# A quarter of w_in loaded earlier and scaled one gate sooner, and two idle matmuls taken out

## The chip, the cores and the metric

The kernel runs on one core of one Trainium2 chip. The metric is the time of one execution on the device in microseconds (us). Six runs of the kernel before gave a median of 107.75 us (107.39 to 110.95; without the highest, 107.39 to 107.86).

## The reference

Two layers follow each other. The first is an attention without softmax: q and k (4 batches, 4 heads, 1088 rows, 32 values) are each projected twice to 8 values, and the outer product of the two projections gives 64 features. The second is a layer with a Swish activation whose slope `beta` differs by hidden unit.

```python
def phi(x):
    a = einsum('rd,bhsd->bhsr', S1, x)
    b = einsum('rd,bhsd->bhsr', S2, x)
    return einsum('bhsi,bhsj->bhsij', a, b).reshape(..., 64)
kv  = einsum('bhsf,bhsd->bhfd', phi(k), v)
z   = sum(phi(k), axis=2)
num = einsum('bhsf,bhfd->bhsd', phi(q), kv)
den = einsum('bhsf,bhf->bhs', phi(q), z)[..., None] + 1e-6
x   = (num / den)            # heads joined: 4352 tokens x 128
h   = x @ w_in               # 128 x 2048
out = (h * (1 / (1 + exp(-beta * h)))) @ w_out   # 2048 x 128
```

The kernel uses that h * sigmoid(beta*h) is silu(beta*h) / beta: it multiplies the columns of w_in by beta and the rows of w_out by 1/beta, and then only needs a plain silu.

## The kernel before

The attention is worked batch by batch. k and q are loaded in rows and transposed in 32x32 blocks on VectorE (`turn_k`, line 378, and `turn_q`, line 384), projected on TensorE, multiplied out to features on VectorE or GpSimd (`outer`, line 441), and summed against v on TensorE (`kv`, line 536). The results for the tokens go as fp16 into `xT`. The second layer then takes tokens in chunks: the first two are of 256 tokens, the others of 512. A "wave" (`w1`, line 332) multiplies one chunk by some columns of the scaled w_in (`winp`), and ScalarE turns the result into `g` with silu; `w2` (line 308) multiplies `g` by the scaled w_out (`woutp`) into `moeout`. With 256 tokens a wave takes 512 columns of winp, that is two slices of 256.

The order on every engine is the order in which the code stands: nothing is reordered by a scheduler. Batch 0 goes first, in code written out by hand (lines 675 to 736), and its q in two parts: "chunk A" is the first 16 of 34 groups of rows, `QA0`, and "chunk B" the other 18. From line 828 a string `SEQ` lists the rest step by step. It begins with `W aB c1 V c0 w4 bB W`: a wave, the spread of chunk B by S1 (`a_B`, line 739), the copy of half of it by ScalarE (`c1`), four matmuls of `w2` (`V`), the other copy, two scalings of w_out, and the spread by S2 (`b_B`).

All large loads are issued by SP's queue in the order of lines 164 to 177. w_in and w_out are loaded in halves. `load_rows(q, ..., ((QA0, T),))` is the second part of q in batch 0, which `turn_q(0, QA0, T)` at line 720 transposes. VectorE has it in its queue ahead of `invert`, which gives the reciprocal `rc` of the denominators of chunk A.

w_in is scaled by GpSimd in slices of 256 columns (`prep_win`, line 257), w_out by ScalarE or GpSimd. GpSimd is held back by "gates" (`gate`, line 671): a copy of one column that waits for a tile of VectorE's. The first gate waits for the last k features of batch 0 (`KP`); one slice follows. The second waits for `rc`; the other seven slices follow.

`keep_warm(n, t)` (line 180) issues n matmuls of 512 columns on a constant tile, whose result nobody reads. In `a_B` two of them write the second of the two PSUM tiles of the spread that comes after. The tiles of tag "wave" turn over two buffers; `nps`, the numerators of chunk A, has the buffer that the first tile of `a_B` takes next.

Of the kernel before, what the change touches and what calls it, by code (L numbers as in the profile page):

```python
# [18 lines left out]
def kernel(  # L19
# [18 lines left out]
    DFF = moe_w_in.shape[1]  # L38
# [3 lines left out]
    T = S // 32  # L42
# [44 lines left out]
    def cut(t, ap, extra=0):  # L87
        return bass.AP(tensor=t.tensor, offset=t.offset + extra, ap=[list(t.ap[0])] + ap)
# [25 lines left out]
    k_t, q_t, v_t = {}, {}, {}  # L114

    def load_rows(src, dst, b, tag, parts=((0, T),)):
        if b not in dst:
            dst[b] = ld.tile([P, T, D], F32, tag=tag, name=tag)
        for t0, t1 in parts:
            nc.sync.dma_start(  # L120
                out=dst[b][:, t0:t1, :],
                in_=bass.AP(
                    tensor=src.tensor,
                    offset=src[b, 0].offset + t0 * D,
                    ap=[[T * D, P], [1, (t1 - t0) * D]],
                ),
            )


    def load_v(b):  # L130
        t = v_t[b] = ld.tile([P, H, NJK, D], F32, tag="v", name="v")
        if b < B - 1:
            for h in range(H):
                nc.sync.dma_start(
                    out=t[:, h],
                    in_=bass.AP(
                        tensor=v.tensor, offset=v[b, h].offset, ap=[[T * D, 32], [NJK * D, 4], [1, NJK * D]]
                    ),
                )
            return  # L140
        nc.gpsimd.memset(t[:, :, NJK - 2 :, :], 0.0)
        for g in range(4):
            nj = min(NJK, T - NJK * g)
            nc.sync.dma_start(
                out=t[g : P : 4, :, :nj],
                in_=bass.AP(
                    tensor=v.tensor,
                    offset=v[b, 0].offset + NJK * g * D,
                    ap=[[T * D, 32], [S * D, H], [1, nj * D]],
                ),  # L150
            )

    def load_win(c0, c1):
        nc.sync.dma_start(out=w_in_sb[:, c0:c1], in_=moe_w_in[:, c0:c1])

    def load_wout(j0, j1):
        nc.sync.dma_start(
            out=w_out_sb[:, j0:j1, :],
            in_=moe_w_out[j0 * P : j1 * P, :].rearrange("(j p) m -> p j m", p=P),
        )  # L160

    K_PARTS = ((0, 18), (18, T))
    QA0 = 2 * q_chk[0][1]
    load_rows(k, k_t, 0, "k", K_PARTS)
    load_rows(q, q_t, 0, "q", ((0, QA0),))
    load_v(0)
    load_wout(0, NJ // 2)
    load_win(0, DFF // 2)
    load_rows(q, q_t, 0, "q", ((QA0, T),))
    load_rows(k, k_t, 1, "k")  # L170
    load_win(DFF // 2, DFF)
    load_wout(NJ // 2, NJ)
# [7 lines left out]
    def keep_warm(n, t=None):  # L180
        if t is None:
            t = pso.tile([P, TCH], F32, tag="moeout", name="warm")
        for _ in range(n):
            nc.tensor.matmul(out=t, lhsT=idle, rhs=cut(idle, [[0, 4], [1, P]]), start=True, stop=True)  # L184
# [72 lines left out]
    def prep_win(c0, c1, eng=None):  # L257
        (eng or nc.gpsimd).tensor_tensor(  # L258
            out=winp[:, c0:c1], in0=w_in_sb[:, c0:c1], in1=beta_bc[:, c0:c1], op=MUL
        )  # L260
# [129 lines left out]
    PS, KP, QO, QT, QP, ND, KAB, QAB, ASB, KVZ, KVD, RB, WZ = ({} for _ in range(13))  # L390

    def wave2(name):
        return psm.tile([P, 2, 512], F32, tag="wave", name=name)

    def two(name):
        return ps2.tile([P, 2, 512], F32, tag="two", name=name)

    def one(name):
        return ps1.tile([P, 512], F32, tag="one", name=name)
# [62 lines left out]
    def spread(which, n, dsts):  # L462
        t0, tn = q_chk[n]
        for c in range(2):
            for m in range(2):
                for pr, dst in enumerate(dsts):
                    h = 2 * pr + m
                    rows = slice(32 * h, 32 * h + 32)
                    nc.tensor.matmul(  # L469
                        out=dst[64 * c : 64 * c + 64, m, : 32 * tn],  # L470
                        lhsT=(sa if which == "a" else sb_)[rows, :],
                        rhs=qT2[0][rows, t0 + c * tn : t0 + c * tn + tn, :],
                        start=True,
                        stop=True,
                    )
# [195 lines left out]
    def gate(t):  # L671
        g = sbA.tile([P, 1], F32, tag="gate", name="gate")
        nc.gpsimd.tensor_copy(out=g, in_=t[:, :1])
# [40 lines left out]
    kvd0 = sb([P, 2, F], F32, "kvd0")  # L714
    nc.scalar.copy(out=kvd0, in_=cut(KVZ[0], [[0, 2], [1, F]]))
    gate(KP[0][:, NJK - 1, H - 1])
    prep_win(0, 256)
    dps = one("dps")
    den0(0, dps)
    turn_q(0, QA0, T)  # L720
# [7 lines left out]
    keep_warm(1, nps[:, 0])  # L728
    num0(0, nps)
    keep_warm(2)  # L730
    for c in range(256, DFF, 256):
        prep_win(c, c + 256)
    for j in range(NJ // 2):
        prep_wout_act(j)
# [3 lines left out]

    def a_B():
        PS["a"] = [wave2("aps"), two("aps")]  # L740
        keep_warm(2, PS["a"][1][:, 0])
        spread("a", 1, PS["a"])

    def b_B():
# [46 lines left out]
    for nm, fn in (("aB", a_B), ("bB", b_B), ("dB", d_B), ("iB", i_B), ("nB", n_B)):  # L791
        DO[nm] = fn
# [76 lines left out]
```

## Time and profile before

| | |
|---|---|
| profiled execution, time | 107.39 us |
| its span, first to last instruction | 105.2 us |
| median of six runs | 107.75 us |
| TensorE busy | 95.9 us (91%) |
| ScalarE busy | 78.0 us (74%) |
| VectorE busy | 66.4 us (63%) |
| GpSimd busy | 26.2 us (25%) |
| mean granted TensorE clock | 0.989 |
| DMA engines busy | nearly full from 4 to 24 us |

Busy time is an average over stages with different limits. The chain of work that ended last follows the program back from its last instruction, at each step to what released it; what stands on it sets the end. The timeline lists the instructions in order of time, and the idle time in front of each, with what ended it. In all views PE is TensorE, PEld its loading of weights, DVE VectorE, ACT ScalarE, POOL GpSimd and SP the queue that issues the loads; `L258` is line 258 of the kernel.

### The profile page before, as it was taken

Reading aid. Unit: us, or ns where it says so; the run is one execution under the profiler, and the core shown is the slowest. Engines: PE = TensorE matmul, PEld = TensorE weight load, DVE = VectorE, ACT = ScalarE, POOL = GpSimd, SP = SyncE. Lnnn points to the kernel's source line nnn. Section 1 sums busy time; section 2 is a strip of 40 time slices with the busy share of each in tenths; the row PEclk is TensorE's granted clock in tenths of the full one; section 3 lists DMA queues with packets and bytes.
Section 4 is the critical chain, followed back from the end, with each engine's and each line's share of the span. In section 5 each row is a group of like instructions: output and inputs, shape, how many; then the busy total and the mean of one; then the engine's idle time right before and its main releaser. Section 6 shows DMA issues by size and latency. Waiting matters only on the chain.

```text
span 105.2 us, 2880 instructions
## 1 busy us (share of the span) xinstructions
PE 95.9 (91%) x1175; PEld 46.0 (44%) x1175; DVE 66.4 (63%) x131; ACT 78.0 (74%) x102; POOL 26.2 (25%) x37
## 2 busy tenths in 40 slices
PE   5778999898979999999999999999899999999930
PEld 2224724355556543534445353346353444445720
DVE  5568998599899935997999564789935200200210
ACT  0648069939897966779977299899892999999920
POOL 5320149640089300400760063008300000000000
PEclk9999999999999999999999999999999999999995
DMA  2999999980002300037800462410014041023043
GB/s 60 310 252 310 363 373 376 418 292 21 6 12 38 55 5 0 6 58 136 329 6 9 81 143 85 82 18 6 0 25 75 0 76 30 0 41 62 15 85 50
DMA packets 24580, 11.33 MB, mean 108 GB/s; under 512 B 18900, under 2 KB 23028, under 8 KB 24568
## 3 DMA queue, kind: packets, MB, share of 16 engines
q1 hardware_dynamic: 23808, 11.05, 37.6%
q8 instruction: 9, 0.15, 0.6%
q10 hardware_dynamic: 696, 0.09, 0.6%
q0 software_dynamic: 64, 0.02, 0.1%
q14 instruction: 3, 0.02, 0.1%
HBM read 8.93 MB, written 2.23 MB: 106 GB/s over the span
## 4 chain that ended last, share of the span: by engine, by line
PE 62%; ACT 17%; DVE 11%; DMA 4%; issue 2%; DVEq 0%; ACTq 0%
PE wave L341 19%; PE moeout L316 19%; ACT g L350 17%; PE kvz L539 5%; PE nps L655 4%; DMA beta<-in_moe_beta_dram 4%; PE kps L406 3%; PE bps L469 2%; PE yps L510 2%; PE aps L469 2%; PE qps L406 1%; DVE rb L614 1%; DVE qT L385 1%; PE betaps L247 1%; DVE xT L634 1%
## 5 line engine op out<-in xcount | busy, mean ns | idle before, releaser
L350 ACT ACTIVATE g<-wave 128x1024 f16<-128x1024 f32 x68 | 65.1, 1037 | 12.0 <-PE wave L341 11.7
L341 PE MATMUL wave<-xT,winp 128*128 128x512 f16 (+1 forms) x160 | 39.7, 347 | 1.3 <-DVE xT L634 0.8
L316 PE MATMUL moeout<-g,woutp 128*128 128x512 f16 (+1 forms) x160 | 38.6, 347 | 0.3 <-ACT g L350 0.3
L341 PEld LDWEIGHTS <-winp 128*128 128x128 f16 x160 | 14.5, 98 | 17.6 <-issue 7.3
L316 PEld LDWEIGHTS <-woutp 128*128 128x128 f16 x160 | 15.0, 97 | 16.1 <-issue 3.5
L326 DVE STREAM_TRANSPOSE o_sb<-moeout 128x512 f32<-128x512 f32 (+1 forms) x10 | 6.2, 620 | 19.6 <-PE moeout L316 19.6
L445 POOL TENSOR_TENSOR qo<-qab 128x512 f32<-128x512 f32 (+1 forms) x7 | 11.0, 1590 | 20.4 <-DVE qab L534 20.4
L445 POOL TENSOR_TENSOR kp<-kab 128x512 f32<-128x512 f32 (+1 forms) x5 | 6.2, 1248 | 16.8 <-DVE kab L428 9.5
L445 DVE TENSOR_TENSOR kp<-kab 128x512 f32<-128x512 f32 (+2 forms) x11 | 8.9, 821 | 0.0
L456 DVE STREAM_TRANSPOSE qt<-qo 128x512 f32<-128x512 f32 (+1 forms) x12 | 8.6, 743 | 0.0
L666 DVE CAST xT<-nps 128x576 f16<-128x576 f32 x5 | 3.8, 758 | 5.6 <-PE nps L655 2.8
L379 DVE STREAM_TRANSPOSE kT<-k 128x1088 f32<-128x1088 f32 (+2 forms) x5 | 5.3, 1067 | 1.1 <-DMA k<-in_k_dram 1.1
L184 PE MATMUL warm<-idle 128*128 128x512 f16 x13 | 4.9, 514 | 1.1 <-DVE idle L96 1.1
L445 DVE TENSOR_TENSOR qo<-qab 128x512 f32<-128x512 f32 (+1 forms) x5 | 5.8, 1192 | 0.1
L258 POOL TENSOR_TENSOR winp<-w_in_sb,beta_bc 128x256 f16<-128x256 f32 x8 | 5.6, 730 | 0.0
L385 DVE STREAM_TRANSPOSE qT<-q 128x1088 f32<-128x1088 f32 (+2 forms) x5 | 5.3, 1065 | 0.4 <-DMA q<-in_q_dram 0.4
L539 PE MATMUL kvz<-kp,v 128*32 128x64 f32 x288 | 5.5, 221 | 0.0
L539 PEld LDWEIGHTS kvz<-kp,v 128*32 128x32 f32 x288 | 4.3, 110 | 2.5 <-issue 1.5
L273 ACT ACTIVATE woutp<-w_out_sb,rbeta 128x128 f16<-128x128 f32 x16 | 5.1, 396 | 0.0
L655 PE MATMUL nps<-qt,nd 32*32 32x288 f32 x192 | 4.8, 412 | 0.0
L428 DVE STREAM_TRANSPOSE kab<-kps 128x288 f32<-128x288 f32 x8 | 3.4, 461 | 1.7 <-PE kps L406 1.7
L486 DVE TENSOR_TENSOR qp<-bps,asb 128x512 f32<-128x512 f32 (+1 forms) x4 | 2.8, 720 | 1.6 <-PE bps L469 1.6
(84 smaller groups left out, 66.9 us busy)
## 6 DMA issues: line engine op xcount, KB each, us to landing
v<-in_v_dram SPq DMA_DIRECT2D x15, 144.0 KB, 4.5
k<-in_k_dram SPq DMA_DIRECT2D x3, 544.0 KB, 7.0
q<-in_q_dram SPq DMA_DIRECT2D x3, 544.0 KB, 7.2
w_out_sb<-in_moe_w_out_dram SPq DMA_DIRECT2D x2, 512.0 KB, 7.7
w_in_sb<-in_moe_w_in_dram SPq DMA_DIRECT2D x2, 512.0 KB, 7.8
out_dram<-o_sb SPq DMA_DIRECT2D x16, 64.0 KB, 1.9
out_dram<-o_sb SPq DMA_DIRECT2D x10, 32.0 KB, 1.6
k<-in_k_dram SPq DMA_DIRECT2D x1, 288.0 KB, 3.2
```

The source lines that it names most:

```text
L258: (eng or nc.gpsimd).tensor_tensor(out=winp[:, c0:c1], in0=w_in_sb[:, c0:c1], in1=beta_bc[:, c0:c1], op=MUL)
L273: nc.scalar.activation(out=woutp[:, j, :], in_=w_out_sb[:, j, :], func=ACTF.Copy, scale=rbeta[:, j : j + 1])
L316: nc.tensor.matmul(out=moe["acc"][:, :tw], lhsT=woutp[:, j, :], rhs=g[jj], start=(j == 0), stop=(j == NJ - 1),)
L326: nc.vector.transpose(out=o_sb[:, :nt, :].rearrange("p t d -> p (t d)"), in_=moe["acc"][:, :tw])
L341: nc.tensor.matmul(out=wv[:, jj // per, o : o + tw], lhsT=winp[:, (j0 + jj) * P : (j0 + jj + 1) * P], rhs=xT[:, t0 : t0 + tw], start=True, ...
L350: nc.scalar.activation(out=g[:, :, :gw], in_=wv[:, :, :gw], func=ACTF.Silu)
L379: nc.vector.transpose(out=kT2[b % 2][:, t0:t1].rearrange("p t s -> p (t s)"), in_=k_t[b][:, t0:t1].rearrange("p t d -> p (t d)"),)
L385: nc.vector.transpose(out=qT2[b % 2][:, t0:t1].rearrange("p t s -> p (t s)"), in_=q_t[b][:, t0:t1].rearrange("p t d -> p (t d)"),)
L445: (eng or nc.vector).tensor_tensor(out=cut(dst[b][:, j0:j1], [[F, n], [R, R], [1, R]]), in0=cut(src[b][:, 0, j0:j1], [[R, n], [1, R], [0, ...
L456: nc.vector.transpose(out=QT[b][:, j0:j1].rearrange("p j h c s -> p (j h c s)"), in_=QO[b][:, j0:j1].rearrange("p j h f -> p (j h f)"),)
L539: nc.tensor.matmul(out=KVZ[b][32 * h : 32 * h + 32, :F], lhsT=v_t[b][:, h, j, :], rhs=KP[b][:, j, h, :], start=(j == 0), stop=(j == NJK - ...
L655: nc.tensor.matmul(out=tiles[g // 2][32 * h : 32 * h + 32, g % 2, :JW], lhsT=ND[b][rows, fc, 32 * h : 32 * h + 32], rhs=QT[b][rows, :, h, ...
```

## The change

There are three edits. In the list of loads, the first half of w_in is cut in two quarters. The first quarter is issued right after v of batch 0, then the second part of q, then the first half of w_out, then the second quarter of w_in. The loads behind these keep their order, and SP issues one load more. At the first gate, GpSimd scales two slices instead of one, and the loop behind the second gate begins one slice later. In `a_B` the two idle matmuls are taken out.

```diff
@@ the loads
     load_v(0)
+    load_win(0, DFF // 4)
+    load_rows(q, q_t, 0, "q", ((QA0, T),))
     load_wout(0, NJ // 2)
-    load_win(0, DFF // 2)
-    load_rows(q, q_t, 0, "q", ((QA0, T),))
+    load_win(DFF // 4, DFF // 2)
     load_rows(k, k_t, 1, "k")
@@ the gate on the k features
     gate(KP[0][:, NJK - 1, H - 1])
-    prep_win(0, 256)
+    for c in (0, 256):
+        prep_win(c, c + 256)
     dps = one("dps")
@@ behind the gate on rc
-    for c in range(256, DFF, 256):
+    for c in range(512, DFF, 256):
         prep_win(c, c + 256)
@@ a_B
         PS["a"] = [wave2("aps"), two("aps")]
-        keep_warm(2, PS["a"][1][:, 0])
         spread("a", 1, PS["a"])
```

## The prediction

> **What bounds the kernel now.** I read the chain of work that ended last first, because it says which stage a saving would have to reach the end from.
>
> ```profile
> PE 62%; ACT 17%; DVE 11%; DMA 4%; issue 2%; DVEq 0%; ACTq 0%
> ```
>
> TensorE carries most of it; ScalarE's 17% is the tail (from 83.16 to 100.69 the chain is one activation after another), and VectorE's 11% lies before 30 us. Both edits lie before 20 us, so next comes the same chain in order of time, there:
>
> ```profile
> 15.58 0.44 DVE xT L634
> 16.02 0.04 issue
> 16.06 0.60 PE wave L341 x4
> 16.66 0.43 PE aps L184 x2
> 17.09 0.90 PE aps L469 x14
> 17.99 0.54 PE moeout L316 x4
> 18.53 1.00 PE bps L469 x12
> ...
> 19.62 0.77 DVE qp L486
> ```
>
> The two idle matmuls that the change removes (`aps L184 x2`) stand on the chain with 0.43 us. That is what they occupy, not yet what they cost. Third, the timeline of that stretch (start, duration, instruction, and in brackets the idle time before it and what ended it):
>
> ```profile
> 12.92 0.73 POOL L258 TENSOR_TENSOR winp<-w_in_sb,beta_bc 128x256 f16<-128x256 f32 x1
> 13.23 0.77 DVE L385 STREAM_TRANSPOSE qT<-q 128x576 f32<-128x576 f32 x1
> 14.05 0.45 DVE L604 STREAM_TRANSPOSE dT<-dps 128x256 f32<-128x256 f32 x1
> 14.53 0.18 DVE L607 TENSOR_SCALAR rc<-dT 128x16 f32<-128x16 f32 x1
> 15.06 0.18 POOL L673 COPY gate<-rc 128x1 f32<-128x1 f32 x1 [1.41 <-DVE rc L608]
> 15.20 4.84 POOL L258 TENSOR_TENSOR winp<-w_in_sb,beta_bc 128x256 f16<-128x256 f32 x7
> 16.39 0.42 DVE L634 TENSOR_TENSOR xT<-nps,rb 128x256 f16<-128x256 f32 x1
> 17.02 0.97 PE L469 MATMUL aps<-qT,s 32*64 32x288 f32 x16
> 18.03 1.18 ACT L480 COPY asb<-aps 128x576 f32<-128x576 f32 x2 [0.22 <-PE aps L469]
> ```
>
> GpSimd stands idle for 1.41 us ahead of the gate on rc. The transpose of q's second part starts with no idle time before it, and the first wave on the chain is released by xT, not by a scaled slice. Last, the windows, for the clock:
>
> ```profile
> 7.90:11.50 3.60, 3.25 (x92) 2.04 (x91) 3.23 (x7) 2.14 (x5) 0.00 (x0) 1.00 0.99 304
> 16.06:19.62 3.56, 3.56 (x44) 1.83 (x44) 1.94 (x3) 3.34 (x8) 3.56 (x6) 1.00 1.06 392
> ```
>
> The seventh figure is the granted clock: 1.00 in both, and the DMA engines beside it are full.
>
> [...] the 128x576 transpose took 772 ns with a GpSimd slice over its first half and 778 ns at 3.95 us with GpSimd idle. On tensor_scalar the trace shows nothing, since none meets a slice. [...] The window 7.90 to 11.50, without one idle matmul, kept 1.00[...].
>
> **The change part by part.** Sums are made against the profiled execution (107.39 us, span 105.2, so 2.19 outside it); it is the lowest of the six, 0.36 under the median of 107.75.
>
> *The idle matmuls.* They go (0.43 us, 16.66 to 17.09). What is late next is a buffer. The first matmul of a_B's spread writes the "wave" buffer that nps held, and nps is read until the second divide ends, 16.39 + 0.42 = 16.81. From the first divide to its wave took 15.58 + 0.42 = 16.00 to 16.06, so 0.06; the spread can then start at 16.87 instead of 17.02. That gives 0.15 of the 0.43; the rest becomes a wait. Behind the spread: the copy c1 on ScalarE (18.03, 0.02 after the spread) comes 0.15 earlier, at 17.88, ScalarE being free at 17.81. The four moeout matmuls need g, which ends at 17.81, so with the same 0.05 or so they move from 17.92 to 17.87, only 0.05. The bps spread follows them. Its second matmul waited for c1 in this execution; in the timeline the sixteen took 1.00 us against 0.97 for the same sixteen of aps, so the wait cost 0.03. The bps spread thus ends 0.05 + 0.03 = 0.08 to 0.09 us earlier and qp on VectorE starts at about 19.53 instead of 19.62. Bounds: 0 (all given back in waits) and 0.15 (the copy alone decides); I take 0.09. From 19.62 to 30 us the chain runs through VectorE and TensorE without a DMA, then TensorE is full, so 0.09 reaches the end.
>
> *The second slice at the kp gate.* No work is added: one 0.73 us slice moves from after the gate on rc to before it. Slices follow each other by 0.69 (15.20, 15.88), so it runs from 13.61 to 14.34, inside the 1.41 us idle. The rc gate behind it opens at 15.01 and isn't delayed. The other six slices end 0.69 sooner, at 19.35 instead of 20.04. Nobody gains: the first wave was held by xT (16.02), and its second slice had ended at 15.93. That cover is 0.09 wide; were xT earlier, the slice would be next, and the change takes that away. [...] bound above 0.65 (the overlap with qT, 0.36, and with dT, 0.29), which the 772 against 778 ns excludes. tensor_scalar begins at 14.53, 0.19 after the slice.
>
> *The loads.* SP issues one load more, of about 0.58 us (the w_in rows: 576 to 579 ns); w_out's first half, k of batch 1 and all behind them are issued about 0.6 us later or more, on one queue with over 1 MB of backlog, so the DMA engines don't starve. Landings: v of batch 0 ends at 8.71, w_out at 10.21, w_in at 12.14, the second part of q at 12.96, which is 1312 KB in 4.25 us, or 309 KB per us. In the new order w_in's quarter (256 KB) is in at about 9.5, q's part (288) at 10.5, w_out (512) at 12.1, w_in's second quarter at 13.0. Wanted: the quarter at 12.92, q at 13.23, w_out by ScalarE's scaling at 14.46, the second quarter by the slice at 15.20. Each has 2 us or more. w_in's packets fall from 4096 to 2048 bytes: 159 and 84 ns in the trace, so 16 x 84 - 8 x 159 = 72 ns more per DMA engine. That reaches k of batch 1 (landed 14.31, wanted 16.73), the second half of w_in (16.48; its slice moves from 17.25 to 16.57, so GpSimd may wait some 0.1 there, for a wave at 22 us) and w_out's second half (18.20, wanted 19.10). All are covered at a cost of 0; without that cover, each costs its lateness. A gain is possible at q: it had only 13.23 - 12.96 = 0.27 us in hand, now 2.7. In the profiled execution that is worth 0.
>
> Sum: -0.09 on the profiled 107.39, or 107.66 on the median; I say 107.65.
>
> **The rivals.**
>
> *q was late in the ordinary execution (107.3).* The profiled execution is 0.36 us under the median. If in the others q's second part comes 0.63 late, VectorE's queue stands still by 0.36 (turn_q is ahead of invert, rc, rb and both divides), and the change removes that: 107.75 - 0.36 - 0.09 = 107.30. For it: 0.27 us in hand behind three large loads on full DMA engines. Against: the profile has no such wait, and the chain begins with the beta load, landing at 5.68, which varies as well and delays everything alike.
>
> [...]
>
> *The clock drops (109 to 110).* [...] Against: a gap of about 0.2 us in 3.56 us, and 1.00 in the window quoted.
>
> *Nothing moves (107.75).* The spread still ends at g's time, and the saved 0.05 to 0.09 is lost in waits. This counts with the forecast.
>
> **How the numbers follow.** About 0.3% (0.32 us) is what a measurement of this kernel tells from no change. Forecast and "nothing moves": 0.47, all within. q late: 0.38, all faster. [...] the clock: 0.05; a load that arrives late, w_out's first half above all: 0.03; together 0.15 slower. The range is 107.2 to 107.95: below lies the further half of the q case, and above the slower cases but for the mildest. The likeliest case's own range is 107.45 to 107.85.
>
> **What would show it.** Right: no idle matmuls ahead of aps, a TensorE gap of about 0.2 us after the first wave ended by xT, aps at 16.87, qp at about 19.53, two slices back to back from 12.92, q's part landed near 10.5, clock 1.00. Wrong: tensor_scalar or a transpose at 14 us longer than 0.18 or 0.77, a wait for w_out ahead of ScalarE's scaling, a clock under 1.00, or a gain over 0.32 us with the timeline moved by only 0.1, which would mean that the executions before the change were held by something that their profile doesn't show.

## The result, and the profile after

The changed kernel takes 107.04 us (median of 37 runs, 106.28 to 108.36); the kernel before, run beside it, 107.85 us (74 runs, 106.89 to 112.13). The ratio is 0.9943, 95% interval 0.9926 to 0.9959: faster by 0.57%, or 0.0057 x 107.85 = 0.61 us. All ratios here leave out executions over 1.5% above the fastest of their kernel, so they stand nearer to one than the medians do; the profiles of `a2_no_idle`, `a3_two_slices`, `c2_q_behind_k` and `c4_fewer_idle_start` fell on such executions, and no ratio rests on them.

The chain that ended last, on the page of the kernel after:

```profile
PE 65%; ACT 17%; DVE 12%; issue 2%; DVEq 0%; ACTq 0%
```

Before it had 4% in DMA, the load of beta. Now there is none: in this execution beta had landed (4.53) before TensorE was through with its first idle matmuls (4.69). The same chain in order of time, over the stretch that was shown of before:

```profile
14.43 0.42 DVE xT L635
...
15.24 0.44 DVE xT L635
15.68 0.14 issue
15.81 1.01 PE aps L470 x15
16.83 0.54 PE moeout L317 x4
17.37 0.99 PE bps L470 x10
...
18.45 0.77 DVE qp L487
```

Everything stands about 1.15 us earlier than before. The distances are as they were: from the first divide (xT) to qp on VectorE it is 18.45 - 14.43 = 4.02 us, and 19.62 - 15.58 = 4.04 before. The 0.43 us of idle matmuls have turned into a wait for the second divide. So this chain gained 0.02 us, and the rest lies further ahead, in what comes earlier in the kernel. The timeline there:

```profile
11.48 0.69 DVE L487 TENSOR_TENSOR qp<-bps,asb 128x512 f32<-128x512 f32 x1
11.77 1.42 POOL L259 TENSOR_TENSOR winp<-w_in_sb,beta_bc 128x256 f16<-128x256 f32 x2
12.08 0.77 DVE L386 STREAM_TRANSPOSE qT<-q 128x576 f32<-128x576 f32 x1
12.90 0.45 DVE L605 STREAM_TRANSPOSE dT<-dps 128x256 f32<-128x256 f32 x1
13.38 0.18 DVE L608 TENSOR_SCALAR rc<-dT 128x16 f32<-128x16 f32 x1
13.91 0.18 POOL L674 COPY gate<-rc 128x1 f32<-128x1 f32 x1 [0.72 <-DVE rc L609]
14.91 0.60 PE L342 MATMUL wave<-xT,winp 128*128 128x256 f16 x4 [0.24 <-DVE xT L635]
16.43 2.09 POOL L259 TENSOR_TENSOR winp<-w_in_sb,beta_bc 128x256 f16<-128x256 f32 x3 [0.97 <-DMA w_in_sb<-in_moe_w_in_dram]
```

Two slices run back to back, the transposes and tensor_scalar take what they took (0.77, 0.45 and 0.18 us), and the first wave is released by xT as before. But q's transpose starts at 12.08, 0.88 us earlier than q's second part had even landed in the profile before (12.96; now 10.78). Had the kernel before been so early in this execution, it would have waited there. The two profiles alone don't prove that this is the gain, since their beginnings differ too: the last of beta's data landed at 5.68 in one and 4.53 in the other.

### The profile page after: what moved, and what is told of

The parts are those of the page before. It is cut to its first block, busy times and chain, and to the rows that moved or that the text cites. A ratio compares the mean times of both kernels' runs of the same rounds, so it can differ in the third digit from the quotient of the medians.

```text
span 104.1 us, 2877 instructions
## 1 busy us (share of the span) xinstructions
PE 95.6 (92%) x1173; PEld 45.8 (44%) x1173; DVE 66.4 (64%) x131; ACT 78.1 (75%) x102; POOL 26.3 (25%) x37
## 3 DMA queue, kind: packets, MB, share of 16 engines
q1 hardware_dynamic: 23952, 11.05, 38.4%
## 4 chain that ended last, share of the span: by engine, by line
PE 65%; ACT 17%; DVE 12%; issue 2%; DVEq 0%; ACTq 0%
PE moeout L317 19%; PE wave L342 19%; ACT g L351 17%; PE kvz L540 5%; PE nps L656 4%; PE warm L185 4%; PE kps L407 3%; PE bps L470 2%; PE yps L511 2%; PE aps L470 2%; DVE rb L615 2%; DVE xT L635 1%; PE qps L407 1%; DVE qT L386 1%; PE betaps L248 1%
```

## The experiments

Three theories: **Q**, q's second part lands too late in ordinary executions of the kernel before; **I**, the idle matmuls; **S** or **W**, the second slice or the early quarter of w_in. There were three series, each beside runs of the kernel before, whose medians were 107.76 us (a), 107.35 (b) and 107.77 (c). Series c ran on another chip than a and b.

**Each part alone.** `a1_loads_only` takes the three lines of loads from the change and nothing else.

```diff
-    load_wout(0, NJ // 2)
-    load_win(0, DFF // 2)
-    load_rows(q, q_t, 0, "q", ((QA0, T),))
+    load_win(0, DFF // 4)
+    load_rows(q, q_t, 0, "q", ((QA0, T),))
+    load_wout(0, NJ // 2)
+    load_win(DFF // 4, DFF // 2)
```

> The new order of the loads alone, one scaled slice at the first gate and the idle matmuls as before. Theory Q (the second part of q lands too late in most executions of the kernel before and holds VectorE's transpose, and so the denominators): all of the gain, ratio 0.993 to 0.996, and in the profile the transpose of q's second part starts right behind the second product qp, with q's part landed near 10.8 us. Theory I (the gain is the idle matmuls) : 1.000. Theory S (the gain is the second slice at the first gate): 1.000.

Measured: 107.16 us, ratio 0.9956 (0.9935 to 0.9977). The loads alone bring the gain, with the idle matmuls still there and one slice at the gate.

`a2_no_idle` takes only the idle matmuls out:

```diff
-        keep_warm(2, PS["a"][1][:, 0])
```

> The idle matmuls of chunk B's first spread alone taken out. Theory Q: 0.999 to 1.000; the two profiles show the spread 0.15 us and 0.20 us after the end of the divide that frees its buffer, so the idle matmuls cost some 0.02 to 0.05 us. Theory I: 0.994 to 0.996. Theory S: 1.000.

Measured: median 109.04 us, ratio 0.998 (0.9953 to 1.0008), no difference that this many runs can tell. The interval still reaches theory I's 0.996; that the gain comes with the idle matmuls in place (`a1_loads_only`, and `a4_q_first` below) speaks against I. The profile is of an execution of 108.95 us:

```profile
14.46 0.73 POOL L258 TENSOR_TENSOR winp<-w_in_sb,beta_bc 128x256 f16<-128x256 f32 x1 [1.39 <-DMA w_in_sb<-in_moe_w_in_dram]
15.08 0.78 DVE L385 STREAM_TRANSPOSE qT<-q 128x576 f32<-128x576 f32 x1 [1.66 <-DMA q<-in_q_dram]
```

This is the wait that the profile of before didn't have: VectorE stands still for 1.66 us for q, and invert and the divides are queued behind. GpSimd waits for w_in beside it. The loads are issued here in the order of the kernel before.

`a3_two_slices` moves only the slice:

```diff
-    prep_win(0, 256)
+    for c in (0, 256):
+        prep_win(c, c + 256)
...
-    for c in range(256, DFF, 256):
+    for c in range(512, DFF, 256):
```

> The second slice of w_in moved ahead of the gate on rc alone. Theory Q: 1.000, since the first wave waits for xT and not for a slice. Theory I: 1.000. Theory S: 0.994 to 0.996.

Measured: median 108.24 us, ratio 0.9993 (0.9965 to 1.0022). S is out. Its profile, of an execution of 110.58 us and again with the loads in the order of before, has q later still:

```profile
15.48 0.78 DVE L385 STREAM_TRANSPOSE qT<-q 128x576 f32<-128x576 f32 x1 [3.11 <-DMA q<-in_q_dram]
```

**q or w_in?** `a4_q_first` is the kernel before with q moved ahead and the weights left in halves, so that w_in comes no earlier than q did:

```diff
+    load_rows(q, q_t, 0, "q", ((QA0, T),))
     load_wout(0, NJ // 2)
     load_win(0, DFF // 2)
-    load_rows(q, q_t, 0, "q", ((QA0, T),))
```

> The second part of q moved ahead of the first halves of w_out and w_in, which stay whole; slices and idle matmuls as before. w_in's half then lands where q landed, near 13 us. Theory Q: the gain, 0.993 to 0.997, with the first slice of w_in late (near 13 us) and GpSimd waiting for it, at no cost or at up to 0.3 us[...]. Theory W (it is w_in's first quarter, late at the first gate, that holds the kernel before, and not q): 1.000 or slower, 1.003.

Measured: 106.89 us, ratio 0.9923 (0.9892 to 0.9953), with w_in as late as Q expected. Its timeline:

```profile
12.36 0.77 DVE L385 STREAM_TRANSPOSE qT<-q 128x576 f32<-128x576 f32 x1
13.12 0.73 POOL L258 TENSOR_TENSOR winp<-w_in_sb,beta_bc 128x256 f16<-128x256 f32 x1 [1.03 <-DMA w_in_sb<-in_moe_w_in_dram]
13.65 0.22 DVE L607 TENSOR_SCALAR rc<-dT 128x16 f32<-128x16 f32 x1
```

GpSimd waits 1.03 us for w_in and the time is none the longer. W is out: what carries the gain is the place of q's second part, which the title doesn't name. Here a slice does run into tensor_scalar, which took 0.22 instead of 0.18 us: 0.04 more, where the last 0.19 us of a slice meet it. But it ended at 13.87, right behind the slice (13.84). What a longer meeting would cost isn't shown.

`b1_q_last` is the opposite: the whole change, but q behind the weights again.

```diff
     load_win(0, DFF // 4)
-    load_rows(q, q_t, 0, "q", ((QA0, T),))
     load_wout(0, NJ // 2)
     load_win(DFF // 4, DFF // 2)
+    load_rows(q, q_t, 0, "q", ((QA0, T),))
```

> The changed kernel with one thing undone: the second part of q goes back behind the first half of w_out and both quarters of w_in; the early quarter, the two slices and the missing idle matmuls stay. Theory Q (q behind 1 MB of weights lands near 13 us or later): the gain is gone, 0.998 to 1.002 of the kernel before, and the transpose of q's second part waits for its load or has it less than 0.5 us ahead. Theory W (w_in's early quarter carries the gain): 0.993 to 0.996.

Measured: 107.58 us, ratio 1.0014 (0.9985 to 1.0044), as theory Q had it. How much this ratio says by itself is taken up below, since the kernel before was faster in this series. The profile is of an execution near the median (107.54 us), and the wait is in it:

```profile
12.32 0.69 DVE L487 TENSOR_TENSOR qp<-bps,asb 128x512 f32<-128x512 f32 x1
...
13.69 0.78 DVE L386 STREAM_TRANSPOSE qT<-q 128x576 f32<-128x576 f32 x1 [0.68 <-DMA q<-in_q_dram]
```

VectorE was free at 13.01 and q landed at 13.66.

**The idle matmuls put back.** `b2_idle_back` is the changed kernel with that line again.

> The changed kernel with the two idle matmuls put back. Theory Q: 0.994 to 0.996 of the kernel before, as the changed kernel; the spread starts 0.20 us after the divide that frees its buffer instead of 0.15. Forecast of the prediction (0.09 us for the idle matmuls): 0.9945 to 0.9965, which these rounds can't tell from Q's. Idle matmuls as the main gain: 0.999 or more.

Measured: 107.19 us, ratio 0.9989 (0.9972 to 1.0006): a miss for Q's number, and close to what the text has for the idle matmuls as the main gain. By this ratio alone that theory could hold. Against it stand `a1_loads_only` and `a4_q_first`, which gained with the idle matmuls in place, and `b1_q_last` of the same series: it lacks them and has q late, and it is slower than `b2_idle_back` by 0.38 us, not faster (averages 107.51 and 107.14 over the executions that enter the ratios; 95% interval of the difference 0.20 to 0.55). So q's place is still worth about 0.4 us here. What the ratio says besides is that the kernel before was 107.35 here, some 0.4 under its other series. The changed kernel itself was not run in this series.

`b4_q_second` puts half of the weights ahead of q:

```diff
-    load_wout(0, NJ // 2)
     load_win(0, DFF // 2)
     load_rows(q, q_t, 0, "q", ((QA0, T),))
+    load_wout(0, NJ // 2)
```

> The kernel before with w_in's half first, then the second part of q, then w_out's half: 512 KB ahead of q instead of 1024. Theory Q: q lands near 11.3 us, ahead of the second product qp, which ends at 12.2 to 13.3 us in the profiles so far; the gain comes whole, 0.992 to 0.997. If any weights ahead of q cost in proportion to their size: half the gain, 0.997. Theory W: w_in's half lands early too, so 0.993 to 0.997; this run does not tell W from Q, q first and q last do.

Measured: 107.21 us, ratio 0.9998 (0.9979 to 1.0017), a miss for all three theories. q landed at 12.36, a microsecond later than worked out, and the transpose still started at 12.94 without a wait. The two kernels of this series with q in time, this one and `b2_idle_back`, took what `a1_loads_only` took in series a (107.16 us), and `b1_q_last` is 0.38 us slower than this one too. It is the kernel before that came out faster in this series. Why isn't shown; it had no profile there.

**What comes next as the bound.** `b3_beta_first` was a try at the beginning: beta's load ahead of S1's.

```diff
+    nc.vector.memset(beta4, 0.0)
     nc.vector.memset(idle, 1.0)
-    nc.vector.memset(beta4, 0.0)
+    nc.scalar.dma_start(out=beta4 ..., in_=moe_beta ...)
     sr = []
     ...
-    nc.scalar.dma_start(out=beta4 ..., in_=moe_beta ...)
```

> The changed kernel with the load of beta issued ahead of that of S1 on ScalarE's queue, and its clearing ahead of the idle tile's. In the profile before, the first matmul that is of use waits for beta, landed at 5.68 us; in the one after, beta is in at 4.53 and the nine idle matmuls at the start end at 4.69. If beta's landing is the next bound: 0.986 to 0.992 of the kernel before, with the first matmul on beta at 4.7 us. If the idle matmuls or S1, now 0.8 us later, take its place: 0.993 to 0.997.

Measured: 108.41 us, ratio 1.0115 (1.0089 to 1.0142), slower than either theory had it. S1 took the place of beta, and not with 0.8 us: it landed at 6.60, where it had landed at 3.86 after the change:

```profile
6.62 0.21 DVE L230 STREAM_TRANSPOSE st<-sr 128x32 f32<-128x32 f32 x1 [2.32 <-DMA sr<-in_S_dram]
```

It stands ahead of k's second transpose (5.09 after the change, 7.35 here), so the projections of k start later.

**The third series** repeats the change beside a dose of the cause.

> The changed kernel itself, beside the other runs of this series. Theory M (the time is the later of two arrivals at VectorE's transpose of q's second part: the end of the second product qp plus 94.05 us, or the landing of that part plus 93.9 us, both from the profiles so far): median 106.9 to 107.2, and the ratio to the kernel before depends on how often q is the later one in this series, 0.993 to 0.999; profile with the product as the later one. If the change had another, fixed gain: 0.994 in every series.

`c1_after_again`, the changed kernel: 106.85 us, ratio 0.9941 (0.9915 to 0.9967), like the result above, and on another chip than series a.

`c2_q_behind_k` has q still later:

```diff
     load_win(0, DFF // 4)
-    load_rows(q, q_t, 0, "q", ((QA0, T),))
     load_wout(0, NJ // 2)
     load_win(DFF // 4, DFF // 2)
     load_rows(k, k_t, 1, "k")
+    load_rows(q, q_t, 0, "q", ((QA0, T),))
```

> The changed kernel with q's second part put behind the first half of w_out, the second quarter of w_in and k of batch 1, so some 1.3 MB later than in the change. Theory M: q lands at 14.8 to 15.5 us and the time is that landing plus 93.9, so 108.7 to 109.4, ratio 1.010 to 1.016, with a wait of 2 us for q ahead of the transpose. If q's landing is hidden, 0.994 to 1.000.

Measured: 109.88 us, ratio 1.0201 (1.0155 to 1.0248): more than theory M had. The timeline has the wait, 2.70 us, and the windows the surplus (the seventh figure is the granted clock):

```profile
15.39 0.78 DVE L386 STREAM_TRANSPOSE qT<-q 128x576 f32<-128x576 f32 x1 [2.70 <-DMA q<-in_q_dram]
```

```profile
14.00:17.60 3.60, 1.19 (x18) 0.38 (x19) 2.00 (x6) 2.27 (x8) 0.54 (x2) 1.00 1.07 364
17.60:24.40 6.80, 6.32 (x60) 2.29 (x59) 3.82 (x6) 3.63 (x6) 3.74 (x6) 0.50 0.96 355
```

While VectorE waits TensorE has little to do, 1.19 of 3.60 us, and then gets half the clock for 6.8 us. This execution took 111.0 us: landing at 15.37 plus 93.9 is 109.3, which leaves 1.7; that this is the slow clock's is an estimate, from the half clock over those 6.8 us. The times of the other five executions go the same way. Four have a mean granted clock of 0.979 to 0.984 and took 109.6 to 110.17 us; the fifth has 0.996, and its 108.84 us lies where theory M had it.

Two tries at a better version. `c3_q_first_all` has q ahead of w_in's quarter:

```diff
+    load_rows(q, q_t, 0, "q", ((QA0, T),))
     load_win(0, DFF // 4)
-    load_rows(q, q_t, 0, "q", ((QA0, T),))
     load_wout(0, NJ // 2)
```

> The changed kernel with q's second part one place further ahead, in front of w_in's first quarter. Theory M: as the changed kernel (q was already ahead of its use there), within 0.002 of it; w_in's quarter lands near 10 us, still ahead of the first gate.

`c4_fewer_idle_start` is that with two idle matmuls fewer at the start:

```diff
-    WARM0 = 9
+    WARM0 = 7
```

> As the one with q first, with seven idle matmuls at the start of the kernel instead of nine. In the profiles the first matmul on beta starts when these end (4.66 to 5.01 us) wherever beta has landed by then. Theory M, with this as what sets the second product: 0.1 to 0.4 us faster than q first with nine. If the clock then comes later, the matmuls behind it take longer (1.66 us instead of 1.14 for those on beta) and it is the same or slower by up to 0.5 us.

Measured: 0.9954 (0.9928 to 0.998) and 0.9954 (0.9914 to 0.9994), medians 107.31 and 107.67 us. Neither beats the change. The first is within 0.002 of its ratio, as theory M had it; for the second the 0.1 to 0.4 us didn't show. In the profile of the second the record of the granted clock begins only at 8.49 us after the first instruction (4.01 in the profile before, 4.17 after), and the matmuls on beta took 2.09 us (1.14 before, 1.21 after):

```profile
5.47 2.09 PE L248 MATMUL betaps<-beta,ones 32*128 32x512 f32 x8 [1.24 <-DVE st L230]
```

That is one execution, and in `a2_no_idle`, with nine idle matmuls at the start, those on beta took 2.1 us. So it isn't shown that the fewer idle matmuls caused it.

**The profiles together.** When the transpose of q's second part starts, and what came last there (in the view a transpose that doesn't wait starts 0.08 to 0.09 us before the product ahead of it ends):

| kernel | second qp ends | q landed | transpose starts | time | time less start |
|---|---|---|---|---|---|
| before | 13.32 | 12.96 | 13.23 | 107.39 | 94.16 |
| after | 12.17 | 10.78 | 12.08 | 106.28 | 94.20 |
| a1_loads_only | 12.90 | 11.18 | 12.82 | 107.00 | 94.18 |
| a4_q_first | 12.44 | 9.22 | 12.36 | 106.48 | 94.12 |
| b1_q_last | 13.01 | 13.66 | 13.69 | 107.54 | 93.85 |
| b2_idle_back | 13.11 | 10.98 | 13.02 | 107.09 | 94.07 |
| b4_q_second | 13.03 | 12.36 | 12.94 | 107.00 | 94.06 |
| b3_beta_first | 14.42 | 11.16 | 14.33 | 108.52 | 94.19 |
| c1_after_again | 12.99 | 11.05 | 12.91 | 107.20 | 94.29 |
| c3_q_first_all | 13.33 | 10.27 | 13.24 | 107.40 | 94.16 |

From the start of that transpose to the end it is 94 us in every row, within 0.44. Nearly all that differs between them lies before it, and the start is the later of two arrivals: the product, whose end wanders from 12.17 to 13.33 (`b3_beta_first` apart) with the beginning of the kernel, or q. Of the four profiles left out, `a2_no_idle` and `c4_fewer_idle_start` have 93.87 and 93.97 in the last column; `a3_two_slices` and `c2_q_behind_k`, with the halved clock, have 95.10 and 95.61. Five kernels with the idle matmuls in `a_B` have 94.06 to 94.18 in the last column. Those without have 94.16 to 94.29, but for `b1_q_last`, where ScalarE had its scaling done during the wait (at 16.58) and g followed its wave at once (16.96 to 16.99). So the idle matmuls cost nothing that this table shows.

Could the new order of loads have hastened the product instead? With q behind the weights it ended between 12.37 and 13.42 in five profiles (two of the table, and those of `a2_no_idle`, `a3_two_slices` and `c2_q_behind_k`), and with q in time between 12.17 and 13.33 in seven. The averages are 12.96 and 12.85. That isn't the gain, though a difference of 0.1 or 0.2 can't be excluded by so few.

By the same table the kernel before, at a median of 107.76 us, starts the transpose at about 107.76 - 94.12 = 13.64 (13.91 with the 93.85 of the kernel that waited), while kernels with q early started at 12.08 to 13.24 (`b3_beta_first` apart). That is where q landed in `b1_q_last` (13.66), and later than the product ended in any row but `b3_beta_first`. It is worked out, an estimate: the one profile of the kernel before itself doesn't have the wait.

## Why the prediction was right or wrong

- *The forecast, 107.65 and no measurable change: it missed the main term.* The change was faster by 0.61 us, where 0.09 was forecast. The measured 107.04 lies just under the range's end of 107.2; taken off the median from which the prediction started, the gain gives 107.75 - 0.61 = 107.14. That the range reached nearly so far was owed to the rival below, not to the forecast's own sum. The step that failed is the last one on the loads: "In the profiled execution that is worth 0." The sentence holds for that execution, and the error was to carry it into the sum for the median, where q's landing was worth most of the 0.61. The execution was the fastest of the six shown, with a late product (13.32) and a q in time (12.96), 0.27 us ahead. Where the product is earlier or q later, q decides.
- *The rival "q was late in the ordinary execution": this is what the runs show.* It had a chance of 0.38. The wait at the transpose was seen (0.68 us in `b1_q_last`, 1.66 in `a2_no_idle`, 3.11 in `a3_two_slices`, 2.70 in `c2_q_behind_k`), and there was none in the kernels with at most 512 KB of weights ahead of q. Moving q alone brought the gain (`a4_q_first`), moving it back cost 0.38 us (`b1_q_last` against `b2_idle_back`, which has the idle matmuls besides), and moving it further back cost 2%. The rival's size was short, 0.45 against 0.61 us. The term that was mis-sized is the 0.36 for the wait, taken as the distance of the profiled execution from the median. That execution was itself late by its product, so the distance hid part of the wait.
- *The idle matmuls: mechanism right, size off.* They did turn into a wait for the nps buffer. Measured from the end of the second divide, the spread moved by about 0.05 and not 0.15: it came 0.15 after the divide (15.66 to 15.81), where 0.06 was taken from the first wave, and 0.20 before. The copy behind it moved by 0.02 (1.20 instead of 1.22 us after the divide). The 0.09 is 0.02 in the profiles and not to be told from 0 in the table.
- *The second slice: right, 0.* The two slices ran back to back from the first gate (11.77 to 13.19), the transpose of q took 0.77 with slices beside all of it, tensor_scalar took 0.18, the first wave waited for xT. One sum for its bound is a little off: a slice up to 14.34 overlaps the transpose of q by 0.39 us and not 0.36; nothing hangs on it.
- *The landings: near.* Worked out 9.5, 10.5, 12.1 and 13.0; measured 9.97, 10.78, 12.21 and 13.59. GpSimd waited 0.97 instead of 0.1 for w_in's second half, since all else was 1.15 earlier; its wave comes later and didn't wait.
- *A slice beside tensor_scalar, a chance of 0.07: an estimate of the author's, and it did not come up.* The second slice ended 0.19 us ahead of tensor_scalar, as worked out. What a meeting would cost isn't shown, since the only one (`a4_q_first`, 0.22 instead of 0.18 us) was with the end of a slice. *The clock*: it stayed at 1.00 without the idle matmuls (14.91 to 18.45), whose gap is 0.3 us; the 109 to 110 of that rival was the author's estimate. It fell to 0.50 in two profiles with q late, after the longest waits (2.70 and 3.11 us), and stayed at 1.00 after 0.68 and 1.66. This is a price of q's lateness that the prediction had in no rival.

Still open: why series b found the kernel before 0.4 us faster than the others did, so that the gain over it shows in series a and c and in the result, but not there.

## What to carry to other kernels

A load that lands 0.3 us ahead of its use in one profile is not hidden: compare it with the spread of both arrivals, and if the profiled execution is the fastest of those shown, take it as the lucky one. Loads on one queue belong in the order in which they are wanted: here the small one that the long chain waits for (288 KB) had to go ahead of the large ones that only a side engine wants (512 KB each). Once it was in time, putting it further ahead (`c3_q_first_all`) brought nothing more. When one stage feeds a long fixed rest, tabulate the start of that stage over all runs: it separates what a change gained from what chance gave. And run the old kernel in every series: a ratio moves with both of its kernels, as series b showed.

## What the runs showed of the hardware

- In two profiles one of a load's sixteen completions came late, and so did one of each load behind it. In the profile of `a2_no_idle` fifteen of the completions of w_out's first half came by 10.52 us and the last at 12.96. w_in behind it had 12.49 and 14.32, q 13.30 and 15.06. VectorE's transpose of q began at 15.08, so after the last. `a3_two_slices` is alike: 11.14 and 13.43, then q 13.78 and 15.46, and the transpose at 15.48. In the profile before no such gap is seen: 10.13 and 10.21 for w_out, 12.09 and 12.14 for w_in, 12.85 and 12.96 for q. What made the one late isn't shown, nor whether it is the same one in each load.
- The granted clock fell to half near 18 us in two profiles, each time after a stretch in which TensorE had little work. In `c2_q_behind_k` it was 0.50 for 6.83 us from 17.63, and in `a3_two_slices` for 3.41 us from 18.28. In the 3.41 us ahead of the drop TensorE was busy for 0.97 us in the first (14.22 to 17.63) and for 0.13 in the second (14.87 to 18.28). In `a2_no_idle` the emptiest 3.41 us (15.35 to 18.76) held 1.27 us of work, and the clock stayed at 1.00. How little work it takes, and over what time, these three don't show.
